# Layer A's normalisers of three chunks spread through DRAM, queries ahead of the output projection, two scratch sets

## The chip, the cores and the metric

The kernel runs on one core of a Trainium2 chip. The core has engines that work side by side and each take their own instructions in order: TensorE (PE, with its weight loads as PEld), VectorE (DVE), ScalarE (ACT), GpSimd (POOL) and SyncE (SP), which here issues the DMA transfers. An instruction that must wait for another engine holds up everything behind it on its own engine. The metric is device time in microseconds of a whole launch; lower is better.

## The reference

The input x has 2048 rows of 1024 values (bf16). Four layers follow one another, A, B, A, B, each with its own layer norm and a residual sum:

```
x = x + A(layernorm(x));  x = x + B(layernorm(x))
x = x + A(layernorm(x));  x = x + B(layernorm(x))
```

Layer A is linear attention with 32 heads of 32 features. Queries and keys go through a small matrix `w_phi` per head; the feature map is the softmax of the result and the softmax of its negative, side by side (64 features):

```
phi_q = concat(softmax(q @ w_phi), softmax(-(q @ w_phi)))      # phi_k alike
kv = sum over rows of phi_k^T v;   z = sum over rows of phi_k
o  = (phi_q @ kv) / (phi_q @ z + 1e-6);   A = o @ wo
```

Layer B is ordinary softmax attention over all 2048 rows, with the same number of heads, and its own `wqkv` and `wo`. The same weights serve both layers A, and both layers B.

## The kernel before

The rows are cut into four chunks of 512 (`c` from 0 to 3); a chunk has four tiles of 128 rows. The residual `xR` stays in SBUF for the whole run. Everything else lives in one SBUF arena of 170 KB per partition, out of which buffers are cut by class, with a quota for each class (`QUOTA`, line 385); PSUM is used as eight banks.

**Who sets the order.** The functions of the kernel don't issue instructions; they hand operations to a planner (`Sched`, lines 62 to 376) with an engine, a duration, what they depend on, their buffers and a priority (a smaller number is more urgent). `Sched.run` lays out a time line by these durations: whenever an engine is free, it takes the ready operation with the smallest priority number for which the buffers can be had. The order that comes out is written into the program and fixed. On the chip every engine follows this order, whether or not the durations hold. A DMA's duration is set by the helper `dma` (line 592): 0.6 us on SP, and a landing 2.25 + kb/210 us later; the broadcasting read below is entered with kb=600.

**One pair of layers**, twice over (`layer` 0 and 1, line 1490). In layer 0 the keys of A are made for all chunks (`a_keys`); in layer 1 only for chunk 3, since the others are made as filler during the attention before (line 1630), along with the query projections of chunk 0 (`q_ahead`, line 943), which wait in DRAM. Then come the queries of A, chunk by chunk at priority `pr = second + 20 * c`:

- `a_queries` (line 959), once for each half `hf` of the eight groups of four heads. PE projects four groups (L600); ACT takes exp of the result and of its negative (L972), which gives the tiles `eq`. PE sums over each head (L983), ACT takes logarithms (L989, L991), DVE subtracts (L993), ACT takes exp (L995): this is the factor `w` by which the negative features have to be scaled, one value for each head and row, held on 8 partitions for each head (16 heads in a half).
- The factor has to stand on all 32 partitions of its head before DVE can multiply. `split_hl` (line 915) writes it as two bf16 parts (L919, L920), and `spread` (line 925) lets PE broadcast these with four matmuls against a selection matrix (L935) into four PSUM banks. DVE multiplies the negative features with them (L1000).
- PE then makes the numerators (L1010), which ACT copies to SBUF (L1014), and the denominators (L1021). ACT takes the denominator's reciprocal by a logarithm and exp (L1026, L1028); `split_hl` and `spread` are used once more, and DVE multiplies the numerators with the result (L1032) into the chunk's output `oc`.
- `a_out` (line 1036) at `pr + PH[1]` projects the output (L600) and adds it to `xR` (L1047); then follow the layer norm for B (`ln_rows`, with transposes through DRAM, L683 and L689), and B's keys and first values at `pr + PH[2]`. With `PH = (1, 22, 43)` and 20 between chunks, chunk c's output projection stands behind the queries of chunk c + 1.

Four chunks, two halves and two normalisers give 16 spreads in each layer A, 32 in all.

**Layer B's attention** (`attention`, line 1183) runs over turns of one chunk and one group. PE makes scores for two or three heads at once (L1209), ACT takes their exp (L1267), and PE multiplies with the values and with ones (L1397). Some score tiles are converted on DVE instead (L1354); `exp_dve` (line 1160) then finishes two of them at a time with bit operations: two masks into the scratch tile `work` (L1171), a product and a sum (L1176). There is one set of `work`, and the planner starts a pair only when the pair before has left it. The quotients of B already go through DRAM: DVE's reciprocals are written to `rd` (L1452) and read back by a DMA that broadcasts four rows to 32 partitions each (L1454), before DVE multiplies (L1459):

```python
bk = dma(prio, lambda r_v=r_v, at_d=at_d: nc.sync.dma_start(
    out=r_v(), in_=at_d.unsqueeze(1).to_broadcast([4, 32, C512])), [aw], [d_b], kb=600)
```

Projections for later groups, the output projection of B (`b_out`, at `P0`, `GAPS`, `OUT_AT`, `GO`) and the keys of the next layer A fill PE's time in between.

## Time and profile before

| | us |
|---|---|
| median of 3 runs (2144.06 to 2144.91) | 2144.25 |
| the profiled execution | 2143.52 |
| its span, first to last instruction | 2141.7 |
| busy in the span: PE, ACT, DVE | 2097.4, 1929.9, 1720.8 |
| first stage of A's queries, about | 147 to 330 |
| second stage of A's queries, about | 1190 to 1365 |

The busy time of PE says little by itself, since matmuls overlap: one lasts some 0.38 us but they start 0.22 us apart. A row of a group has the line, the engine, the operation, output and input tiles with shapes, the count, busy time and mean duration in ns, and the idle time of the engine just before these instructions with what ended it. In a chain of waits each row is a piece of the work that ended last: start, length, what it was. A stretch's row has the busy time of each engine in it, the granted TensorE clock, the mean busy share of the 16 DMA engines, and GB/s.

### The profile page before, as it was taken

How to read it: one execution, taken by the hardware profiler on the slowest of the kernel's cores; microseconds unless marked ns; L12 is line 12 of the kernel's file. 1: busy time of each engine (PE TensorE's matmuls, PEld its weight loads, DVE VectorE, ACT ScalarE, POOL GpSimd, SP SyncE). 2: the span in 40 equal slices, each digit the busy share in tenths (PEclk: the TensorE clock that was granted, in tenths of full speed). 3: DMA queues.
4: the chain of work that ended last, by engine and by line, in shares of the span. 5: the costliest groups of instructions: out<-in, count | busy, mean ns of one | idle time of the engine just before them, and what ended most of it. 6: DMA issues, size and time to landing. Idle time of an engine off the chain costs nothing.

```text
span 2141.7 us, 64212 instructions
## 1 busy us (share of the span) xinstructions
PE 2097.4 (98%) x27375; PEld 795.1 (37%) x27437; DVE 1720.8 (80%) x3151; ACT 1929.9 (90%) x2044; POOL 27.4 (1%) x78
## 2 busy tenths in 40 slices
PE   8999999999999999999999999999999999999999
PEld 5543443333333333333333434533333333333333
DVE  8876553665567899997887876599899999999998
ACT  7437668999999999999999576799999999999998
POOL 1000000000000000000000000000000000000000
PEclk9999999999999999999999999999999999999999
DMA  7820321112233431451456212211111122311111
GB/s 233 164 71 20 86 63 32 32 42 49 65 99 85 123 107 52 120 154 47 108 154 194 78 40 69 70 28 31 36 49 38 45 53 54 84 39 52 54 44 37
DMA packets 255271, 160.73 MB, mean 75 GB/s; under 512 B 147592, under 2 KB 229512, under 8 KB 254984
## 3 DMA queue, kind: packets, MB, share of 16 engines
q1 hardware_dynamic: 254984, 156.62, 27.3%
q8 instruction: 214, 3.51, 0.7%
q14 instruction: 73, 0.60, 0.1%
HBM read 89.72 MB, written 29.87 MB: 56 GB/s over the span
## 4 chain that ended last, share of the span: by engine, by line
PE 57%; ACT 26%; DVE 9%; issue 5%; DMA 2%; POOL 0%; SPq 0%; ACTq 0%; DVEq 0%; POOLq 0%
ACT arena L1267 26%; PE psum L600 19%; PE psum L604 13%; PE psum L1397 11%; PE psum L1209 10%; DVE arena L1354 3%; DVE work L1171 1%; PE psum L1010 1%; DVE work L1176 1%; DVE arena L1176 1%; DMA arena<-rd 1%; DMA arena<-arena 1%; PE psum L855 1%; ACT arena L820 1%; PE psum L935 1%
## 5 line engine op out<-in xcount | busy, mean ns | idle before, releaser
L1267 ACT ACTIVATE arena<-psum 128x1536 bf16<-128x1536 f32 (+1 forms) x1343 | 1580.5, 1478 | 4.7 <-PE psum L1209 2.9
L604 PE MATMUL psum<-arena 128*32 128x512 bf16 (+1 forms) x9536 | 633.1, 365 | 4.2 <-DVE arena L816 1.0
L1397 PE MATMUL psum<-arena 128*32 128x512 bf16 x4096 | 607.5, 382 | 1.9 <-DVE arena L1412 1.6
L1397 PE MATMUL psum<-arena,ones_bf 128*32 128x512 bf16 x4096 | 607.7, 382 | 0.0
L1209 PE MATMUL psum<-arena 32*128 32x512 bf16 x4096 | 527.2, 383 | 25.7 <-ACT arena L1267 20.6
L1354 DVE TENSOR_SCALAR arena<-psum 128x512 uint16<-128x512 f32 x610 | 415.1, 686 | 117.6 <-PE psum L1209 112.9
L600 PE MATMUL psum<-arena 128*128 128x512 bf16 (+1 forms) x1916 | 429.6, 372 | 4.3 <-issue 1.8
L1209 PEld LDWEIGHTS <-arena 32*128 32x128 bf16 x4096 | 161.1, 91 | 559.2 <-issue 555.2
L604 PEld LDWEIGHTS <-arena 128*32 128x32 bf16 x9536 | 206.1, 95 | 255.3 <-issue 161.9
L600 PEld LDWEIGHTS <-arena 128*128 128x128 bf16 x1968 | 186.4, 98 | 215.4 <-issue 17.1
L1397 PEld LDWEIGHTS <-arena 128*32 128x32 bf16 x4096 | 167.2, 95 | 211.6 <-issue 144.0
L1171 DVE TENSOR_SCALAR work<-arena 128x1024 uint16<-128x1024 uint16 (+1 forms) x616 | 237.7, 418 | 5.7
L1176 DVE TENSOR_TENSOR arena<-work 128x1024 bf16<-128x1024 bf16 (+1 forms) x308 | 209.9, 682 | 5.5
L1176 DVE TENSOR_TENSOR work<-arena,work 128x1024 bf16<-128x1024 bf16 (+1 forms) x308 | 209.1, 679 | 0.1
L1397 PEld LDWEIGHTS <-ones_bf 128*32 128x32 bf16 x4096 | 165.9, 95 | 19.1 <-issue 3.3
L820 ACT ACTIVATE arena<-psum 128x512 bf16<-128x512 f32 x80 | 43.6, 595 | 74.4 <-PE psum L600 61.5
L1073 DVE CAST arena<-psum 128x512 bf16<-128x512 f32 (+1 forms) x120 | 69.5, 579 | 41.0 <-PE psum L604 41.0
L824 DVE TENSOR_REDUCE arena<-arena 128x32 f32<-128x1024 bf16 x64 | 77.6, 1213 | 21.4 <-ACT arena L820 21.0
L1412 DVE COPY arena<-psum 128x512 f32<-128x512 f32 x126 | 86.3, 685 | 10.0 <-PE psum L1397 9.8
L972 ACT ACTIVATE arena<-psum 128x512 bf16<-128x512 f32 x112 | 62.0, 605 | 30.4 <-PE psum L600 26.0
L833 DVE TENSOR_TENSOR arena<-psum,arena 128x1024 bf16<-128x1024 f32 x64 | 78.1, 1222 | 5.3 <-PE psum L604 3.1
L645 ACT ACTIVATE arena<-xR 128x1024 bf16<-128x1024 bf16 x40 | 42.3, 1058 | 30.9 <-DVE xR L1047 30.2
(99 smaller groups left out, 1048.4 us busy)
## 6 DMA issues: line engine op xcount, KB each, us to landing
arena<-in_B_wqkv_dram SPq DMA_DIRECT2D x66, 256.0 KB
arena<-rd SPq DMA_DIRECT2D x62, 256.0 KB
xa<-arena SPq DMA_DIRECT2D x48, 256.0 KB
arena<-in_A_wqkv_dram SPq DMA_DIRECT2D x40, 256.0 KB
arena<-in_B_wo_dram SPq DMA_DIRECT2D x40, 256.0 KB
arena<-arena SPq DMA_DIRECT2D x256, 32.0 KB
arena<-wd_k SPq DMA_DIRECT2D x32, 256.0 KB
arena<-arena SPq DMA_DIRECT2D x62, 128.0 KB
```

The source lines that it names most:

```text
L600: nc.tensor.matmul(out_, lhsT=lhsT, rhs=rhs, start=start, stop=stop, skip_group_check=True)
L604: nc.tensor.matmul(out_[ks, :], lhsT=lhsT[:, ks], rhs=rhs, start=start, stop=stop, tile_position=(0, 32 * k), skip_group_check=True)
L824: red = op("DVE", dve_us(1024) + 0.107, lambda ev=ev, sv=sv: nc.vector.reduce_sum(out=sv(), in_=ev().rearrange("p s (h d) -> p (s h) d", d ...
L833: ml = op("DVE", dve_us(1024), lambda vpv=vpv, wv_=wv_, sv=sv: nc.vector.tensor_tensor(out=wv_()[:, :, :, 0:DH], in0=vpv().rearrange("p (h ...
L1073: return soon(op("DVE", dve_us(n), lambda: nc.vector.tensor_copy(out=dst(), in_=src()), [dep], bufs, prio))
L1171: return sch.later("DVE", n * C512 / 3840 + 0.065, lambda: nc.vector.tensor_scalar(out=out_().bitcast(U16), in0=y_v().bitcast(U16), scalar ...
L1176: return sch.later("DVE", n * C512 / 1920 + 0.065, lambda: nc.vector.tensor_tensor(out=out_(), in0=in0(), in1=in1(), op=what), deps, [e_b, ...
L1209: nc.tensor.matmul(out=out_, lhsT=kT[g][1]()[r, pp, d * P:(d + 1) * P], rhs=q_of[(qc, g)][1]()[r, (pp + j // 2) % 2, :], start=True, stop= ...
L1267: ex = make("ACT", act_us(w * C512), lambda: nc.scalar.activation(out=e_v()[:, 0:w * C512], in_=s_v()[:, 0:w * C512], func=ACT.Exp, scale= ...
L1354: pair["got"].append(sch.later("DVE", dve_us(512), lambda: nc.vector.tensor_scalar(out=e_v().bitcast(U16)[:, k, :], in0=s_v(), scalar1=EXP ...
L1397: nc.tensor.matmul(out=a_v()[col:col + 32, :], lhsT=v_v()[:, kc % 4, o:o + DH] if what == 0 else ones_bf[:], rhs=ev()[:, x * C512:(x + 1) ...
L1412: cp = op("DVE", dve_us(512), lambda t_v=t_v, a_v=a_v: nc.vector.tensor_copy(out=t_v(), in_=a_v()), [last], [a_b, t_b], prio - 4)
```

## The change

- `send` is new: the factor (`w`, or the denominator's reciprocal) is written to a DRAM scratch `rw`, one partition of each eight, 16 rows in one DMA; four DMAs then read four rows each, broadcast to 32 partitions a row, into float32 tiles `bw` in SBUF. It takes the place of `split_hl` and `spread` for chunk 0 of layer 0 and chunks 0 and 1 of layer 1 (`FAR = (1, 2)`). DVE's multiplies (L1000, L1032) then read `bw` instead of PSUM.
- `PH` becomes `(1, 42, 63)`: a chunk's output projection and what follows it stand one chunk of queries later.
- `work` has two sets, and two pairs of `exp_dve` may be under way at once. The arena shrinks from 170 to 166 KB. Quotas for `eq`, `ns` and `cw` grow, and `bw` gets 16.
- Some of the planner's durations for short DVE operations are lower, some priorities of filler work move (`QT`, `OUT_AT`, `GO`, `GAPS`), one limit goes from 0 to 1 (`MOST`), and the planner's search through SP's ready list ends early once priorities lie beyond its window; an assertion is added.

```diff
@@ Sched.run
+            assert t < 4000.0
...
+                    if e == "SP" and item[1] > todo[front] + WINDOW:
+                        skipped.append(item)
+                        break
@@ constants
-SBUF_ARENA = 170 * 1024
+SBUF_ARENA = 166 * 1024
...
-         "eq": 12, "ns": 4, "cw": 6, "hl": 6, "oc": 2, "slab": 8, "slabk": 3, "fin": 4,
+         "eq": 20, "ns": 12, "cw": 12, "hl": 6, "oc": 2, "slab": 8, "slabk": 3, "fin": 4,
...
-QT = (188, 300, 310)
+QT = (194.22, 300, 310)
...
+FAR = (1, 2)
...
-OUT_AT = (233.27, 240.45, 284.45)
-GO = 2.34
+OUT_AT = (233.27, 253.5, 284.45)
+GO = 2.55
...
-PH = (1, 22, 43)
+PH = ((1, 42, 63), (1, 42, 63))
...
-GAPS = (1.5, 2.47, 2.87)
+GAPS = (1.5, 2.47, 1.81)
...
-MOST = (lambda i: 0 if i < 1 else 12, lambda i: 16 if i < 1 else 29)
+MOST = (lambda i: 1 if i < 1 else 12, lambda i: 16 if i < 1 else 29)
@@ the kernel
-    work = const.tile([P, 2, max(NB), C512], BF16, tag="work")
+    work = const.tile([P, 2, 2, max(NB), C512], BF16, tag="work")
...
+    rw = dram_p.tile([32 * 16, C512], F32, tag="rw")
+    rw_v = rw[:].rearrange("(t h) n -> t h n", h=16)
+    sent = []
@@ beside spread
+    def send(r_b, r_v, dep, prio):
+
+        at_d = rw_v[len(sent)]
+        sent.append(prio)
+        aw = dma(prio, lambda: nc.sync.dma_start(out=at_d, in_=r_v()[0:P:8, :]), [dep], [r_b], kb=32)
+        got = []
+        for a in range(4):
+            b, v = sb("bw", C512, dt=F32)
+            got.append((b, v, dma(prio + 0.001 * a, lambda a=a, v=v: nc.sync.dma_start(
+                out=v(), in_=at_d[4 * a:4 * a + 4].unsqueeze(1).to_broadcast([4, 32, C512])), [aw], [b], kb=600)))
+        return got
@@ a_queries
-        h_b, h_v, h = split_hl(lm_b, lm_v, w, prio)
         ew, nums = [], []
-        for a, (b_, v_, bm) in enumerate(spread(h_b, h_v, h, prio)):
+        for a, (b_, v_, bm) in enumerate(send(lm_b, lm_v, w, prio) if c < away else spread(*split_hl(lm_b, lm_v, w, prio), prio)):
...
-        k_b, k_v, k = split_hl(r_b, r_v, l4, prio)
-        for a, (b_, v_, bm) in enumerate(spread(k_b, k_v, k, prio)):
+        for a, (b_, v_, bm) in enumerate(send(r_b, r_v, l4, prio) if c < away else spread(*split_hl(r_b, r_v, l4, prio), prio)):
@@ exp_dve
-        x_b = Buf("ps", 0, "xx", [(8,)])
+        x_b = Buf("ps", 0, "xx", [(8,), (9,)])
...
-        x_v = lambda: work[:, 0, 0:n, :]
-        p_v = lambda: work[:, 1, 0:n, :]
+        x_v = lambda: work[:, x_b.at[0] - 8, 0, 0:n, :]
+        p_v = lambda: work[:, x_b.at[0] - 8, 1, 0:n, :]
```

More of the change, by code (lines that the diff above doesn't have):

```diff
@@ L641, in ln_rows @@
                     for h in range(2)]
-                sums.append(op("DVE", 0.2, lambda t=t, b_v=b_v: nc.vector.bn_aggr(
+                sums.append(op("DVE", 0.12, lambda t=t, b_v=b_v: nc.vector.bn_aggr(
                     out=s_v()[:, 2 * t:2 * t + 2], in_=b_v().rearrange("p (h s) -> p h s", s=6)), bn, [b_b, s_b], prio))
@@ L957, in q_ahead, with a_queries @@
                     out=qf_v[:, c, g, :], in_=f_v()), [cp], [f_b], kb=256)
-    def a_queries(c, hf, prio, wq_s, state, o_chunk):
+    def a_queries(c, hf, prio, wq_s, state, o_chunk, away):
         xb, xv, fin = xnA[c]
@@ L1421, in attention @@
                     o_b, o_v = sb("oT", C512)
-                    rc = [op("DVE", 128 * 8 / 960 + 0.12, lambda b=b, T=T, r_v=r_v: nc.vector.reciprocal(
+                    rc = [op("DVE", 128 * 8 / 960 - 0.2, lambda b=b, T=T, r_v=r_v: nc.vector.reciprocal(
                         out=r_v()[hi_, b * P:(b + 1) * P], in_=T[0][1]()[hi_, b * P:(b + 1) * P]),
@@ L1450, in attention @@
                     [T[k][2]], [c_b, T[k][0]], kb=2) for k in range(2) for i in range(2)]
-                rc = op("DVE", 0.27, lambda c_v=c_v: nc.vector.reciprocal(out=c_v(), in_=c_v()), m, [c_b], prio)
+                rc = op("DVE", 0.17, lambda c_v=c_v: nc.vector.reciprocal(out=c_v(), in_=c_v()), m, [c_b], prio)
                 aw = dma(prio, lambda c_v=c_v, at_d=at_d: nc.sync.dma_start(
@@ L1544 @@
             for hf in range(2):
-                a_queries(c, hf, pr + PH[0] * hf, wq_s, state, oc)
-            a_out(c, pr + PH[1], wo_s, oc)
-            xnB[c] = ln_rows(c, 1 + 2 * layer, pr + PH[1] + 1, LN_DVE[layer], c >= LN_PE[layer], c >= LN_PE[layer])
-            b_k(0, c, pr + PH[2], wk0, kT, ANY, "ACT")
+                a_queries(c, hf, pr + PH[layer][0] * hf, wq_s, state, oc, FAR[layer])
+            a_out(c, pr + PH[layer][1], wo_s, oc)
+            xnB[c] = ln_rows(c, 1 + 2 * layer, pr + PH[layer][1] + 1, LN_DVE[layer], c >= LN_PE[layer], c >= LN_PE[layer])
+            b_k(0, c, pr + PH[layer][2], wk0, kT, ANY, "ACT")
             if c == 0:
-                q_of[(0, 0)] = b_q(0, 0, pr + PH[2] + 0.5, wq0, ANY)
+                q_of[(0, 0)] = b_q(0, 0, pr + PH[layer][2] + 0.5, wq0, ANY)
             for t in range(TB):
-                b_v(0, c, t, pr + PH[2] + 1 + 0.1 * t, bv_s[0], vT, ANY, "ACT", (0,) if HALF[layer] else (0, 1))
+                b_v(0, c, t, pr + PH[layer][2] + 1 + 0.1 * t, bv_s[0], vT, ANY, "ACT", (0,) if HALF[layer] else (0, 1))
         gate = []
```

6 lines of the change are left out of this document (3 added, 3 removed).

## The prediction

> **What bounds the kernel now.** I read the page first, then busy time by stage, then the chain of waits inside one stage.
>
> ```profile
> span 2141.7 us, 64212 instructions
> PE 57%; ACT 26%; DVE 9%; issue 5%; DMA 2%; POOL 0%; SPq 0%; ACTq 0%; DVEq 0%; POOLq 0%
> ```
>
> The profiled execution took 2143.52 us around this span; the runs' median, 2144.25, is 0.7 above it. One average hides two regimes, so the second view cuts the span into layer A's query stages (147 to 330 and 1190 to 1365) and the attention stages behind them (columns: stretch, length, busy time of PE, PEld, DVE, ACT, POOL, clock, DMA share, GB/s):
>
> ```profile
> 147.00:330.00 183.00, 181.35 (x1115) 77.64 (x1133) 99.49 (x198) 125.34 (x240) 0.00 (x0) 1.00 0.20 51
> 330.00:1170.00 840.00, 823.04 (x12192) 281.76 (x12191) 631.92 (x1119) 837.19 (x731) 10.14 (x25) 1.00 0.33 90
> 1190.00:1365.00 175.00, 173.58 (x1213) 79.88 (x1232) 117.60 (x219) 113.94 (x225) 2.58 (x8) 1.00 0.21 56
> 1365.00:2141.70 776.70, 760.29 (x11007) 269.33 (x11005) 733.00 (x1393) 763.86 (x678) 0.00 (x0) 1.00 0.17 46
> ```
>
> In the query stages PE is busy for 354.9 of 358 us, while ACT and DVE rest for a third: TensorE sets the pace. In attention ACT has no hole in layer one (837.19 of 840) and only the tail's 12.8 us in layer two. So PE work taken out of a query stage comes off the end, and so does every hole put into it. The change's new operations all lie there. The chain inside the first query stage agrees:
>
> ```profile
> 149.76 5.13 PE psum L600 x23
> 207.04 5.34 PE psum L600 x24
> 244.43 10.74 PE psum L600 x49
> ```
>
> Its long pieces are projections on PE; no transfer is among them. What the change puts there is a transfer.
>
> **The change part by part.**
>
> *TensorE's spreads go.* Three chunks, each with two halves and two normalisers: 12 spreads of 4 matmuls. What one costs, from the order of time:
>
> ```profile
> 1253.17 3.19 PE L600 MATMUL psum<-arena 128*128 128x512 bf16 x14
> 1256.29 0.39 PE L935 MATMUL psum<-arena,selb 32*128 32x512 bf16 x4
> 1256.62 0.60 PE L600 MATMUL psum<-arena 128*128 128x512 bf16 x2
> ```
>
> Fourteen projections keep a pitch of 0.216 us (10.74 us for 49, less one pipeline depth, gives the same), so the last starts at 1255.98; the next one starts at 1256.62, 0.64 later. Without the spread it would be 0.216: a spread costs 0.42. Twelve give 5.1 us; with the whole 0.64 each, 7.7. I take 5.1, the row's own difference.
>
> *VectorE's splitting goes.* 12 casts and 12 subtractions:
>
> ```profile
> L919 DVE CAST arena<-arena 128x512 bf16<-128x512 f32 x32 | 13.6, 425 | 32.2 <-ACT arena L1028 28.8 <-ACT arena L995 3.2
> L920 DVE SCALAR_TENSOR_TENSOR arena<-arena,hl 128x512 bf16<-128x512 bf16 x32 | 24.0, 749 | 0.7
> L1000 DVE TENSOR_TENSOR arena<-arena,psum 128x512 bf16<-128x512 bf16 x64 | 39.9, 683 | 6.5 <-PE psum L935 6.5
> L1459 DVE TENSOR_TENSOR arena<-arena 128x512 bf16<-128x512 f32 x62 | 42.6, 687 | 7.0 <-DMA arena<-rd 5.8 <-DMA arena<-qd 0.8 <-PE psum L1209 0.2
> ```
>
> 12 x (0.425 + 0.749) = 14.1 us of DVE, worth nothing where DVE rests for 84 and 57 us. The 48 multiplies that now read float from SBUF instead of PSUM cost the same (0.683 and 0.687).
>
> *Queries ahead of output projection* (21 to 42 priority units later). No work changes; it can only fill PE's holes, 1.65 + 1.42 us in the two stages. Zero, bound -3.1.
>
> *Two scratch sets.* The attention's groups, and DVE's holes before the last two steps of its exponential (last columns: busy us, mean ns | idle before):
>
> ```profile
> L1267 ACT ACTIVATE arena<-psum 128x1536 bf16<-128x1536 f32 x801 | 1196.3, 1650 | 4.0 <-PE psum L1209 2.2 <-DMA xa<-arena 1.1 <-PE psum L1397 0.6
> L1267 ACT ACTIVATE arena<-psum 128x1024 bf16<-128x1024 f32 x541 | 619.6, 1223 | 0.7 <-PE psum L1209 0.7
> ...
> L1354 DVE TENSOR_SCALAR arena<-psum 128x512 uint16<-128x512 f32 x610 | 415.1, 686 | 117.6 <-PE psum L1209 112.9 <-issue 0.7 <-ACT arena L820 0.4
> L1171 DVE TENSOR_SCALAR work<-arena 128x1024 uint16<-128x1024 uint16 x604 | 234.8, 421 | 5.7
> L1176 DVE TENSOR_TENSOR arena<-work 128x1024 bf16<-128x1024 bf16 x302 | 207.4, 687 | 5.3
> ```
>
> At most 11 us of DVE. Time falls only if units move from ACT to DVE; one costs DVE 0.69 + 0.42 + 0.69 = 1.8 us (conversion, and half of two masks and two combines), so six, at 0.43 us of ACT each (1.650 against 1.223 for three and two banks): -2.6. The limits per turn are the same (0 and 1 alike refuse a pair of two), so I take 0.
>
> *4 KB less arena, retimed fillers, the planner's durations.* Same instructions in another order. ACT's rest in attention, 2.8 + 12.8 us, bounds a gain; nothing bounds a loss. I take 0, and +-3 for the range. The planner's new break and assertion issue nothing.
>
> *The way through DRAM.* Per send: one write of 16 rows, then four reads that each broadcast 4 rows to 128 partitions. The kernel already has that read, form for form, for layer B's normalisers:
>
> ```profile
> 1095.24 3.23 DMA rd<-arena
> ...
> 1098.52 6.20 DMA arena<-rd
> ...
> 1104.81 0.69 DVE arena L1459
> ```
>
> Write 3.28 us to the read's issue; read 6.2 until DVE may use it. The helper that orders the work assumes 0.6 + 2.25 + 600/210 = 5.7 for it, and reads issued 0.6 apart, so an order in which four pieces arrive 5.7, 6.3, 6.9 and 7.5 us after the first issue. For one read that is nearly right. Four together are not in the trace: the closest two are 11.5 us apart:
>
> ```profile
> 907.46 0.57 SPq L1454 DMA_DIRECT2D arena<-rd  x1
> ...
> 918.95 0.59 SPq L1454 DMA_DIRECT2D arena<-rd  x1
> ```
>
> But the read can be seen from within. Two that nothing disturbs, from 1.4 us after their issue (the first one's row), beside the opening loads:
>
> ```profile
> 992.57 0.60 SPq L1454 DMA_DIRECT2D arena<-rd  x1
> ```
> ```profile
> 0.00:50.00 50.00, 43.78 (x467) 28.85 (x474) 41.77 (x80) 34.70 (x65) 5.96 (x19) 0.97 0.82 248
> 993.97:997.12 3.15, 3.15 (x49) 1.08 (x49) 2.55 (x5) 3.15 (x4) 0.00 (x0) 1.00 0.21 81
> 2095.24:2098.50 3.26, 3.06 (x46) 1.08 (x38) 3.23 (x7) 3.26 (x4) 0.00 (x0) 1.00 0.22 79
> ```
>
> 3.15 us at 81 GB/s is 255 KB, one read; share 0.21 of 16 engines is 3.4 of them, where the opening loads use 13. So a read lives on about four engines and fills them for 3.2 us. Ends for four reads: side by side on other engines, as the order assumes (last piece at 6.2 + 1.8 = 8.0), or in single file on the same four (6.2, 9.4, 12.6, 15.8). I take single file: four reads of one form and one queue have nothing to set their engines apart. The last piece then is 8.3 us later than its place in the order, and engines wait in order.
>
> The Trainium skill says this outright (DMA: Bandwidth & Descriptors, Queues, rings and completion order): a copy is split over the largest k up to 16 that divides the outermost sizes of both sides, here 4 and 128, and on the queues of SP the lowest-numbered k are used. The share of 0.21 agrees with k = 4; by the page single file is certain, by the share alone it is likely.
>
> What waits behind a late piece: on DVE the multiply (L1000, L1032), and all that DVE has queued behind it; on PE the numerator (L1010) after L1000. Where each first half and normaliser becomes ready:
>
> ```profile
> 157.21 0.65 ACT L995 ACTIVATE arena<-arena 128x512 f32<-128x512 f32 x1
> 159.78 2.48 DVE L1000 TENSOR_TENSOR arena<-arena,psum 128x512 bf16<-128x512 bf16 x4 [0.67 <-PE psum L935]
> ```
> ```profile
> 176.30 0.69 ACT L1028 ACTIVATE arena<-arena 128x512 f32<-128x512 f32 x1
> ```
> ```profile
> 1189.03 0.65 ACT L995 ACTIVATE arena<-arena 128x512 f32<-128x512 f32 x1
> ```
> ```profile
> 1215.16 0.68 DVE L1000 TENSOR_TENSOR arena<-arena,psum 128x512 bf16<-128x512 bf16 x1
> ```
> ```profile
> 1226.41 0.63 ACT L1028 ACTIVATE arena<-arena 128x512 f32<-128x512 f32 x1
> ```
> ```profile
> 1265.66 0.63 ACT L1028 ACTIVATE arena<-arena 128x512 f32<-128x512 f32 x1
> ```
>
> Layer one, chunk 0: ready 157.9, reads from 161.1. Sixteen reads in file end at 161.1 + 51.2 + 3.0 = 215.3. In the order, the last send starts 7 us later than at 177.0 now (the multiply comes 8.9 after readiness instead of 1.9), and ends 3.3 + 7.5 later: 194.8. So it is between 8.3 (one send's tail) and 20.5 late. Layer two: the first send is covered (ready 1189.7, used at 1215.16). From 1227.0 six sends follow: 1230.3 + 76.8 + 3.0 = 1310.1 against 1265.7 + 7 + 10.8 + 0.6 = 1284.1 for the last: between 8.3 and 26.0 late. PE has no rest to win it back; DVE has a third of its time. I take the middles, 14.4 + 17.2 = 31.6, since DVE catches up on part and PE needs only half of the sends at once.
>
> SP issues 60 transfers more and waits for each write before its reads:
>
> ```profile
> L1454 SPq DMA_DIRECT2D arena<-rd x62: 573/590/662, 368.0 to 2116.1; - x62
> ```
> ```profile
> L1452 SPq DMA_DIRECT2D rd<-arena x62: 320/333/1614, 366.4 to 2114.7; - x62
> ```
> ```profile
> SPq L1454 <- DMA rd<-arena: 31.9, 36, 2.8
> ```
>
> That is 12 x 0.33 + 48 x 0.59 = 32 us of issue and up to 2.8 of waiting per send, ahead of the layer norm's writes and transposes (L683, L689) and the weight slabs. Those are needed a chunk later, and the moved output projections delay the layer norms as well: 0.
>
> Sum: 2143.5 - 5.1 + 31.6 = 2170.0; plus 0.7 for the median: 2171.
>
> **The rivals.**
> *Faster, side by side.* If a read takes whatever engines are free, the last piece is 0.5 us late and the order holds: 2144.25 - 5.1, and up to 3.1 of PE's holes: 2137. For it: a quarter of the engines leaves three quarters idle, at share 0.2. Against: the one form and queue. It decides where a send's four reads land within 8 us. Chance 0.27.
> *Covered.* Single file, but one more chunk of projections (64 x 0.216 = 13.8 us) lies ahead of the first output projection, and only one send's tail reaches PE: 2144.25 - 5.1 + 3 = 2142. For it: layer two's first send waits 25 us anyway. Against: a finished half has the smallest priority number, so its numerator goes next on PE. Chance 0.10, half of it within 0.2%.
> *Full file.* Both upper ends, seven sends in layer two (42 instead of 26): 2144.25 - 5.1 + 20.5 + 42 = 2202. For it: DVE in order. Against: DVE's rest. Holes of 2.6 us between pieces may also slow the clock, which is 1.00 in all four stages and 0.97 in the first 50 us. Chance 0.14. The Trainium skill (TensorE: Matmul & The Clock Gate, Part 1) has the clock halved after an idle window of about 3.4 us; by that, single late pieces alone would not do it, and this trace has no such hole.
> *Attention reordered.* The smaller arena holds back a buffer, or the fillers' new places leave ACT without scores; ACT's 0.43 us per unit is lost for each such unit. +3 to +10, 2150, without any stall for the detour; or the reverse, 2138. Chance 0.07.
>
> **How the numbers follow.** About 0.2% (4 us) is what a measurement of this kernel tells from no change. The forecast has 0.42 (2156 to 2190 its own range), full file 0.14, covered 0.10, side by side 0.27, attention 0.07. Faster: 0.27 + 0.04 + 0.02 = 0.33, one part of it within 0.2%, so 0.32. Same: 0.06. Slower: 0.42 + 0.14 + 0.06 = 0.62. The range reaches to side by side below (2134 with PE's holes and 3 us of order) and towards full file above (2194).
>
> **What would show it.** Right: the reads of the new tensor land about 3 us apart; DVE's L1000 and L1032 have idle time ended by DMA, over 20 us together; PE shows holes before L1010; in layer one the stage behind 147 grows by over 8 us. L935 shrinks from 128 to 80 matmuls and L919 and L920 from 32 to 20 whatever happens. Wrong: L1000 waits under 1 us for its pieces, a stretch over a send has a DMA share near 0.8, and the stages shrink by 2 to 4 us each.

## The result and the profile after

The changed kernel took 2224.16 us (median of 4 runs, 2222.37 to 2226.54) against 2144.58 before: a ratio of 1.037, 95% interval 1.0352 to 1.0388, 79.6 us slower. The forecast was 2171, 26.5 us above the kernel before, with a range up to 2194: the sign is right, the size three times too small.

The page of the changed kernel, its span and the shares of the chain that ended last:

```profile
span 2220.3 us, 64211 instructions
...
PE 48%; ACT 30%; DVE 8%; DMA 7%; issue 6%; SPq 1%; POOL 0%; ACTq 0%; DVEq 0%; POOLq 0%
```

The transfers' share of the chain rose from 2% to 7%, TensorE's fell from 57% to 48%. By stretch (columns as in the prediction: PE, PEld, DVE, ACT, POOL, clock, DMA share, GB/s), with both query stages taken to their new ends:

```profile
147.00:350.00 203.00, 186.85 (x1136) 77.82 (x1134) 95.53 (x190) 129.74 (x242) 0.00 (x0) 0.97 0.23 66
350.00:1193.00 843.00, 822.66 (x12155) 283.32 (x12151) 619.28 (x1099) 833.77 (x727) 10.23 (x25) 1.00 0.32 88
1193.00:1440.00 247.00, 206.49 (x1383) 87.21 (x1380) 129.78 (x239) 133.74 (x263) 2.88 (x8) 0.91 0.36 103
1440.00:2220.30 780.30, 764.08 (x11008) 273.09 (x11006) 712.32 (x1378) 766.13 (x682) 0.00 (x0) 1.00 0.18 45
```

Two things are new, and both are in the query stages. TensorE stands still for 203 - 186.85 = 16.2 us in the first and 40.5 in the second, where it stood 1.65 and 1.42. And its clock, 1.00 in both before, is 0.97 and 0.91, which is worth 0.03 x 203 = 6.1 and 0.09 x 247 = 22.2 us. Together 85 against 3: that is where the 80 us are. The sum counts some 7 us twice, since the clock is also low within some holes (0.63 in the one from 1333.94 to 1341.99, where TensorE stands still anyway); counted once it is 57 of holes and 21 of slow clock, 78.

VectorE's multiplications with the first factors that come through DRAM (order of time; start, length, idle time before):

```profile
165.68 0.69 DVE L1019 TENSOR_TENSOR arena<-arena 128x512 bf16<-128x512 bf16 x1 [9.06 <-DMA arena<-rw]
168.28 0.69 DVE L1019 TENSOR_TENSOR arena<-arena 128x512 bf16<-128x512 bf16 x1 [1.91 <-DMA arena<-rw]
170.85 0.69 DVE L1019 TENSOR_TENSOR arena<-arena 128x512 bf16<-128x512 bf16 x1 [1.89 <-DMA arena<-rw]
173.45 0.69 DVE L1019 TENSOR_TENSOR arena<-arena 128x512 bf16<-128x512 bf16 x1 [1.90 <-DMA arena<-rw]
```

and SP's queue, which sends them:

```profile
157.94 0.58 SPq L953 DMA_DIRECT2D rw<-arena  x1
160.42 4.26 SPq L957 DMA_DIRECT2D arena<-rw  x4
176.33 5.01 SPq L953 DMA_DIRECT2D rw<-arena  x2
181.45 11.89 SPq L957 DMA_DIRECT2D arena<-rw  x8
```

The four reads of a send land 2.6 us apart: single file, as forecast. The next two sends start only at 176.33, 18 us after the first, and both at once, so that eight reads stand in one file. The groups of waits (total, times, longest):

```profile
DVE arena L1050 <- DMA arena<-rw: 50.4, 17, 8.5
DVE arena L1019 <- DMA arena<-rw: 43.0, 20, 9.1
...
PE psum L1029 <- DVE arena L1019: 13.3, 3, 6.3
...
PE psum L608 <- DVE arena L1050: 10.5, 8, 2.2
ACT arena L992 <- DMA rw<-arena: 10.4, 7, 2.5
```

VectorE waits 93 us for pieces, and TensorE waits for VectorE: the numerators (L1029) and denominators (L1040) for the first factors, the output projections (L608) for the second ones. These waits are 32 of the 57 us of holes. Another 14.2 are query projections (also L608) that wait for ScalarE's exponentials (L992) to free a bank, mostly where ScalarE had itself waited for a send's write to land (10.4 us in the last row above; 8.2 us more, once, ahead of the layer norm, L653). In the second stage, TensorE's own rows, of which the last, the longest hole, is of this second kind:

```profile
1279.05 0.59 PE L1029 MATMUL psum<-arena 128*128 128x512 bf16 x1 [6.28 <-DVE arena L1019]
...
1304.35 0.39 PE L608 MATMUL psum<-arena 128*128 128x512 bf16 x1 [1.46 <-DVE arena L1050]
1306.92 0.61 PE L608 MATMUL psum<-arena 128*128 128x512 bf16 x1 [2.19 <-DVE arena L1050]
...
1341.99 3.57 PE L608 MATMUL psum<-arena 128*128 128x512 bf16 x8 [8.05 <-ACT arena L992]
```

### The profile page after: what moved, and what is told of

Same layout as the page of the kernel before. It is cut to its first block, busy times and chain, and to the rows that moved or that the text cites. A ratio compares the mean times of both kernels' runs of the same rounds, so it can differ in the third digit from the quotient of the medians.

```text
span 2220.3 us, 64211 instructions
## 1 busy us (share of the span) xinstructions
PE 2121.4 (96%) x27372; PEld 799.2 (36%) x27372; DVE 1679.8 (76%) x3095; ACT 1935.2 (87%) x2046; POOL 27.5 (1%) x78
## 4 chain that ended last, share of the span: by engine, by line
PE 48%; ACT 30%; DVE 8%; DMA 7%; issue 6%; SPq 1%; POOL 0%; ACTq 0%; DVEq 0%; POOLq 0%
ACT arena L1285 27%; PE psum L612 13%; PE psum L608 13%; PE psum L1415 10%; PE psum L1227 9%; DMA arena<-rw 4%; DVE arena L1372 2%; SPq L957 1%; DVE work L1189 1%; DMA rw<-arena 1%; DVE work L1194 1%; DVE arena L1194 1%; PE psum L863 1%; DMA arena<-arena 1%; ACT arena L828 1%
## 5 line engine op out<-in xcount | busy, mean ns | idle before, releaser
L1415 PE MATMUL psum<-arena 128*32 128x512 bf16 x4096 | 613.8, 382 | 4.7 <-issue 2.2
L1372 DVE TENSOR_SCALAR arena<-psum 128x512 uint16<-128x512 f32 x598 | 407.4, 687 | 125.8 <-PE psum L1227 114.4
L608 PE MATMUL psum<-arena 128*128 128x512 bf16 (+1 forms) x1968 | 452.2, 382 | 25.7 <-ACT arena L992 14.2
L608 PEld LDWEIGHTS <-arena 128*128 128x128 bf16 x1968 | 189.7, 100 | 273.3 <-issue 68.9
L1189 DVE TENSOR_SCALAR work<-arena 128x1024 uint16<-128x1024 uint16 x606 | 240.3, 419 | 3.2
L1194 DVE TENSOR_TENSOR arena<-work 128x1024 bf16<-128x1024 bf16 x303 | 205.9, 680 | 2.9
L1194 DVE TENSOR_TENSOR work<-arena,work 128x1024 bf16<-128x1024 bf16 x303 | 205.8, 679 | 0.0
L992 ACT ACTIVATE arena<-psum 128x512 bf16<-128x512 f32 x112 | 61.9, 606 | 45.9 <-PE psum L608 24.2
L1033 ACT COPY arena<-psum 128x512 f32<-128x512 f32 x64 | 38.0, 594 | 54.7 <-PE psum L1029 39.4
L653 ACT ACTIVATE arena<-xR 128x1024 bf16<-128x1024 bf16 x40 | 42.4, 1061 | 49.1 <-DVE xR L1065 40.9
```

Source lines behind the costliest of these rows:

```text
L608: nc.tensor.matmul(out_, lhsT=lhsT, rhs=rhs, start=start, stop=stop, skip_group_check=True)
L1189: return sch.later("DVE", n * C512 / 3840 + 0.065, lambda: nc.vector.tensor_scalar(out=out_().bitcast(U16), in0=y_v().bitcast(U16), scalar ...
L1194: return sch.later("DVE", n * C512 / 1920 + 0.065, lambda: nc.vector.tensor_tensor(out=out_(), in0=in0(), in1=in1(), op=what), deps, [e_b, ...
L1372: pair["got"].append(sch.later("DVE", dve_us(512), lambda: nc.vector.tensor_scalar(out=e_v().bitcast(U16)[:, k, :], in0=s_v(), scalar1=EXP ...
L1415: nc.tensor.matmul(out=a_v()[col:col + 32, :], lhsT=v_v()[:, kc % 4, o:o + DH] if what == 0 else ones_bf[:], rhs=ev()[:, x * C512:(x + 1) ...
```

## The experiments

Ratios are to the kernel before, on the same chip; "after" is the changed kernel. The constant QT is a due time of the planner; where a version needed another value for the planner to find an order, the diff shows it. The edits are shown in part: quotas of new buffer classes and the size of the DRAM scratch are left out.

**How much is the detour: no chunk, or layer one's alone.**

```
e1  -FAR = (1, 2)  -QT = (194.22, ...)
    +FAR = (0, 0)  +QT = (200, ...)
e5  -FAR = (1, 2)
    +FAR = (1, 0)
```

> The changed kernel with FAR = (0, 0): no chunk goes through DRAM, all the rest of the change stays. (QT is 200 instead of 194.22, because the planner finds no order at 194.22 once the sends are gone.) Theory 1, the four reads of a send run in file on the same few DMA engines and their late pieces stall VectorE and TensorE: both query stages shrink to about 185 and 200 us, no idle time of L1019 or L1050 ends with a DMA, the granted clock is 1.00 again, the time is 2135 to 2160. Theory 2, the new order of queries, the smaller arena and the moved fillers cost most: 2190 or more.

> The changed kernel with FAR = (1, 0): one chunk in layer 0 goes through DRAM, none in layer 1. Theory 1: layer 0's stage stays as long as in the changed kernel (exponentials of attention start near 340 instead of 319), layer 1's stage goes back to some 200 us from 242, and the piece that spilled into the second attention comes back too: 2224 less about 49, 2170 to 2180. Theory 2: over 2195, since the other parts are all there.

Without any detour 2151.15 (1.0033, interval 1.002 to 1.0045); with layer one's chunk alone 2168.35 (1.0114, 1.01 to 1.0128). So the detour costs 73 us, 17 of them by layer one's chunk and 56 by layer two's two; the rest of the change costs 6.8. QT is 200 in e1 and 194.22 in e5 and the kernel after, and no run has its effect alone: the 56 is a difference at one value, the 73, the 17 and the 6.8 are not. e1 lies in theory 1's range, e5 just below it. The query stages without detour have no hole and a full clock:

```profile
147.00:350.00 203.00, 202.96 (x1400) 84.45 (x1397) 105.56 (x206) 142.75 (x253) 0.32 (x1) 1.00 0.18 48
1176.00:1378.00 202.00, 201.95 (x1486) 93.24 (x1477) 135.16 (x252) 136.93 (x273) 2.59 (x8) 1.00 0.30 84
```

**Does layer two's price come from two chunks running into each other?**

```
e14 -FAR = (1, 2)  -QT = (194.22, ...)
    +FAR = (0, 1)  +QT = (200, ...)
```

> FAR = (0, 1): only the first chunk of layer two goes through DRAM. One chunk in layer one alone took 2168, 17 us over none at all (2151); the other two chunks of layer two then took 56. Theory of a price for each send (holes of the same size, chunk by chunk): 2172 to 2182, half of the 56. Rival (the two chunks of layer two run into each other, their sends in one file): 2160 to 2170, like the chunk of layer one, or less because its first send is covered.

2176.62 (1.0146, 1.0131 to 1.0161): 25.5 us for one chunk of layer two, near half of the 56, in the theory's range. The price goes by chunk (e1 and e14 have the same QT). The second stage, the only one touched:

```profile
1175.00:1402.00 227.00, 208.26 (x1474) 94.62 (x1470) 131.34 (x245) 136.80 (x273) 2.59 (x8) 0.96 0.33 94
```

18.7 us of holes and 0.04 x 227 = 9.1 of slow clock. That is somewhat more than layer one's chunk pays (16.2 and 6.1), and half of what the pair pays.

**The landing: four wide reads to a send.** Each read now fills 32 partitions with all four pieces, its 32 repeats outermost; a piece is complete when all four reads have landed.

```
e3  -b, v = sb("bw", C512, dt=F32)                      # one of four
    -out=v(), in_=at_d[4 * a:4 * a + 4].unsqueeze(1).to_broadcast([4, 32, C512])
    +b, v = sb("bw", 4, C512, dt=F32)                   # all four
    +out=v()[32 * h:32 * h + 32], in_=at_d.rearrange("(a h) n -> h a n", h=4)[h].unsqueeze(0).to_broadcast([32, 4, C512])
```

> The changed kernel with the same bytes read in another cut: each of a send's four reads fills 32 partitions with all four pieces, with the 32 repeats as the outermost size, so that it can use 16 DMA engines instead of about 4. Theory 1 (file on few engines): the last piece lands within 8 us of the first issue instead of about 13, a stretch over a send has a DMA share of 0.5 or more, waits of L1019 and L1050 for the reads fall from 93 us to under 25, the clock stays at 1.00 nearly throughout, the time is 2130 to 2160. Theory 3 (any way through DRAM is too long for this order, whatever its rate): waits stay over 60 us and the time over 2190.

2185.92 (1.0203, 1.0189 to 1.0217): the same bytes, 38 us less. Both ranges were missed: VectorE's waits for the reads fell from 93 to 54 us, not below 25. SP's and VectorE's rows of the first send:

```profile
159.03 0.58 SPq L953 DMA_DIRECT2D rw<-arena  x1
161.10 2.20 SPq L955 DMA_DIRECT2D arena<-rw  x4
```
```profile
168.44 2.50 DVE L1018 TENSOR_TENSOR arena<-arena 128x512 bf16<-128x512 bf16 x4 [10.73 <-DMA arena<-rw]
```

All four pieces are there 7.3 us after the first read's issue; in the kernel after the last came at 173.45, 13.0 after its first issue. A stretch within the reads, first of the kernel after, then of this one:

```profile
163.00:170.00 7.00, 7.00 (x29) 2.92 (x27) 1.38 (x2) 3.44 (x7) 0.00 (x0) 0.84 0.26 102
```
```profile
163.00:167.00 4.00, 4.00 (x20) 1.85 (x19) 0.00 (x0) 2.17 (x4) 0.00 (x0) 1.00 0.96 219
```

A quarter of the DMA engines at 102 GB/s, against nearly all of them at 219. The Trainium skill (DMA: Bandwidth & Descriptors, Why a DMA increments its semaphore by 16 and not by 1) splits a copy over the largest k up to 16 that divides the slowest dimensions of both sides; with 4 outermost the trace shows a share of 0.26, near 4 of 16; with 32 outermost, 0.96. Row and rule agree. The stages of this version:

```profile
147.00:350.00 203.00, 194.09 (x1255) 81.67 (x1257) 95.52 (x191) 143.62 (x254) 0.32 (x1) 1.00 0.28 66
1180.00:1398.00 218.00, 198.06 (x1429) 87.05 (x1426) 128.57 (x239) 129.60 (x258) 2.85 (x8) 0.98 0.47 122
```

Holes of 8.9 and 19.9 us, about half of those of the kernel after, and only 4.4 of slow clock.

**Is it an order made for landing times that are too short?** e4 makes the planner count 2.6 us for each broadcasting read, one behind the other (layer B's too); e15 (built on e10, below) adds 3 us to each such read.

```
e4  +if pick.file:
    +    self.narrow = max(self.narrow, t + 1.4) + 2.6
    +    land = max(land, self.narrow + 1.5)
    -QT = (194.22, ...)
    +QT = (198, ...)
e15 -land = max(land, self.wire + 0.6)
    +land = max(land, self.wire + 0.6) + 3.0 * pick.file
```

> The changed kernel, its narrow reads unchanged, but the planner counts them as the trace shows them: one after another, 2.6 us each, the first from 1.4 us after its issue, 1.5 us more to land (for layer B's reads too). QT is 198. Theory 1a, what costs is the order's error: the planner fills the wait with other work, few holes on TensorE, 2140 to 2165. Theory 1b, the file itself costs (48 reads of 2.6 us are 125 us, and too little other work is ready): holes on TensorE remain, 2185 to 2225.

2239.97 (1.0446, 1.0432 to 1.046), slower than the kernel after and above both ranges. A truer plan does not pay.

**Is it the series of the two halves?** In the kernel after the second half's first write comes 18 us or more behind the first half's. The planner hands the buffers of a class out strictly by priority, so the second half's sums wait for a bank that the first half's denominators take first. e6 and e7 give the denominators' bank a class of its own, with narrow and with wide reads:

```
e6, e7  -d_b, d_v = ps("cmp", ANY)
        +d_b, d_v = ps("dn", ANY)
e6      -QT = (194.22, ...)
        +QT = (200, ...)
```

> The changed kernel, narrow reads, with one edit in the planner's classes: the denominators' PSUM bank gets a class of its own, so that the sums of the second half need not wait in the order until the first half's denominators have their bank. (QT is 200.) In the changed kernel the factor of chunk 0's second half is ready 23 us after the first's (156.7 and 179.7), before the change 9.3. Theory H, the sends of the two halves stand in series and each adds its whole way to the chain: now the second factor comes some 10 us after the first, sends overlap, DMA waits of L1019 and L1050 fall below 70 us, 2185 to 2210. Theory F, the file of narrow reads is the bound by itself: over 2212.

> The same class edit together with the reads on 16 engines. If series and file together are the whole cost of the way through DRAM: DMA waits under 25 us, stages as in the run without the detour (attention from about 321, second gap about 202), 2140 to 2160. If something else of the detour costs (SP's order, landing times): over 2170, as with the wide reads alone.

2242.19 (1.0447, 1.0431 to 1.0463) and 2188.26 (1.0196, 1.0181 to 1.0211): no gain, as the rivals had it. But a second lock of the same kind had remained. In e7 the second half's first logarithm (L1008) still comes right behind the first half's denominators' (L1044), whose tile is in the same class:

```profile
172.94 0.60 ACT L1044 ACTIVATE arena<-psum 128x512 f32<-128x512 f32 x1
173.44 0.59 ACT L1008 ACTIVATE arena<-psum 128x512 f32<-128x512 f32 x1
```

So e10 (on e3) and e11 (on the kernel after) free that tile and the second send's landing buffer as well; e12 does it to the kernel before.

```
e10, e11, e12  -d_b, d_v = ps("cmp", ANY)         +d_b, d_v = ps("dn", ANY)
               -r_b, r_v = sb("cw", C512, dt=F32) +r_b, r_v = sb("cwr", C512, dt=F32)
e10, e11       -send(r_b, r_v, l4, prio)          +send(r_b, r_v, l4, prio, "bwr")
```

> The kernel after with wide reads, and with three buffers taken out of the classes in which the planner hands buffers out strictly in order of priority: the denominators' PSUM bank, the denominators' SBUF tile, and the landing buffer of the second send. So the second half's sums, its logarithms, its write and its reads no longer stand behind those of the first half's denominators. Theory (the two halves' sends stand in series because of these orders, and the holes of that series slow the clock): the two halves' first writes come 8 to 11 us apart instead of 23, layer A's first stage (first exponentials of attention 0) falls from 326.4 in the wide version to 318 to 324, the query stage of layer 1 from 218.6 to 203 to 210, total 2150 to 2168. Rival (the price is the landing time itself, each send leaves its hole whatever the order of the halves): first stage 324 or more, total 2180 to 2195, as with wide reads and with the denominators' bank alone.

> The same three buffers in classes of their own, but the reads as in the kernel after, four narrow ones to a send. Theory of the series: the halves overlap, but the eight reads of two sends stand in one file of 2.6 us each, so a part of the price stays: first stage 326 to 334, total 2172 to 2195, that is, about what the prediction had forecast with its overlapped file (2171). Rival (the order of the halves is beside the point): total 2210 to 2235.

> The kernel before with the denominators' bank and tile in classes of their own, no detour. In the kernel before the halves' first writes of the small tile stand 9 us apart already, and the stage is bound by TensorE: theory, nothing is gained, 2140 to 2152. Rival (the order of the halves costs time without any detour too): 2125 to 2138.

2200.27 (1.0255, 1.0238 to 1.0272), 2232.18 (1.0408, 1.0392 to 1.0423) and 2161.41 (1.0076, 1.0061 to 1.0091). In e10 the halves do overlap, with writes 10 us apart:

```profile
158.52 0.58 SPq L953 DMA_DIRECT2D rw<-arena  x1
161.14 2.82 SPq L955 DMA_DIRECT2D arena<-rw  x4
168.45 0.49 SPq L953 DMA_DIRECT2D rw<-arena  x1
```

and yet it is 14 us slower than e3, and e11 8 slower than the kernel after; the other order alone costs the kernel before 16, which neither range for e12 held. e10 lies above both of its ranges, e11 in the rival's. My theory falls: the series is there, but undoing it wins nothing. What it may win by itself can't be told apart from the 16 us that the other order costs.

> The version with wide reads and the three buffers in classes of their own, and the planner is told 3 us more for each read, so that it puts the multiplications where they can run on the chip (write to multiplication 11.7 us in its plan; measured 11.9). Theory (a send is late only because the order was made for times that are too short, other work for TensorE is there): layer two's query stage falls from 232.8 to under 212, total under 2172. Rival (there is no other work within reach, the hole stays wherever the order puts the send): stage 218 or more, total 2180 to 2205.

2198.93 (1.0248, 1.0232 to 1.0263), as e10 and in the rival's range. Its second stage has 20.1 us of holes with the longer times in the plan:

```profile
1182.00:1425.00 243.00, 222.89 (x1746) 101.58 (x1745) 132.59 (x244) 138.21 (x273) 4.29 (x9) 0.97 0.46 119
```

**Is it the slow clock?** Six matmuls on old data ahead of each numerator that waits for a sent factor, in an unchanged order; the numerator overwrites them.

```
e13 +WARM_MM = 6
    +for _ in range(WARM_MM if c < away else 0):
    +    nc.tensor.matmul(n_v(), lhsT=kvm()[:, 2 * g, :], rhs=kvm()[:, 0:4, :].rearrange("p a b -> p (a b)"), start=True, stop=True)
```

> The kernel after, in the same order, with six more matmuls on old data (1.3 us at full clock) on TensorE ahead of each of the 24 numerators whose factor comes through DRAM; the numerator overwrites what they write. In all 31 us of TensorE work that nothing needs, put where the holes are. Theory (about a third of the price, half of the 65 us in which the clock stands at half, comes from the holes slowing the clock): the time at half clock falls from 65 to under 30 us, and the kernel is faster for the added work, 2195 to 2216. Rival (the clock is low only while TensorE waits anyway, and costs nothing): time at half clock falls as well, but the total stays or grows, 2224 to 2255.

2229.12 (1.039, 1.0373 to 1.0408), 5 us above the kernel after:

```profile
147.00:350.00 203.00, 191.38 (x1170) 81.57 (x1171) 95.75 (x190) 128.99 (x240) 0.00 (x0) 0.99 0.22 66
1192.00:1442.00 250.00, 220.05 (x1466) 95.57 (x1467) 128.80 (x237) 131.91 (x260) 2.87 (x8) 0.95 0.36 100
```

My range was missed, the rival's held. The slow clock fell from about 28 us' worth to 2.0 + 12.5, and the holes from 57 to 41.6, but the 31 us of added work took both gains (six matmuls 0.216 us apart, 24 times). That the clock's part would be won if the holes were filled with useful work is not shown.

**Is it a false wait on the write?** In e10 ScalarE's next exponential waits for the write at 10 of the 12 sends. e16 (on e10) and e17 (on the kernel after) keep the small tile until the reads have landed, in case its memory is what the exponential gets. When the wait stayed, e18 (on the kernel after) and e19 (on e16) wrote the whole tile, not every eighth partition.

```
e16, e17       -... [aw], [b], kb=600)
               +... [aw], [b, r_b], kb=600)
e18, e19       -dma_start(out=at_d, in_=r_v()[0:P:8, :])
               +dma_start(out=at_d, in_=r_v())
e18            -in_=at_d[4 * a:4 * a + 4]
               +in_=at_d[32 * a:32 * a + 32:8]
```

> The version with wide reads and three classes of their own, and the small tile that a send writes from is handed back only when the reads have landed, not when the write is planned to be done. In the version without this the next exponential of a query (ScalarE) takes that memory and waits for the write: 25.0 us in 10 waits of ScalarE, 2 to 3.5 us at every send. Theory (this reuse is where the holes come from once the halves overlap): the waits of the exponentials on the write go, first stage under 325, query stage of layer two under 217, total 2160 to 2180. Rival (ScalarE waits then for something else in the same chain; the landing itself is the price): 2190 to 2205.

> The kernel after with the same longer hold on the small tile, nothing else changed. There the exponentials waited 10.4 us in 7 waits on the write, the multiplications 93 us on the reads. Theory (reads in file, one send behind the other, make the price of the kernel after): within 10 us of it, 2214 to 2234. Rival (the reuse of the tile makes the order): under 2205.

> The kernel after in the same order, but a send writes its whole tile (128 rows, 256 KB) to DRAM and the reads pick their 16 rows there. In the kernel after the write takes every eighth partition of the tile; next behind each of the 12 writes ScalarE and VectorE wait for it to land, though they write to other memory. Theory A (the strided source is taken for the whole on-chip memory, so that each write stops the two engines; that is a part of the price): the exponentials' waits on the write (10.4 us in 7) go, total 2196 to 2214. Theory B (those waits lie inside the waits for the reads, 93 us, which stay): 2216 to 2228.

> The version with overlapped halves, wide reads and the longer hold (2183), with the whole tile written. There ScalarE and VectorE wait for each write too, the multiplications of the first half for the write of the second. Theory A: those waits (ScalarE 25.2 us in 10, VectorE 25 us in 7) go, and with them what was left of the price: first stage 320 to 324, query stage of layer two under 210, total 2148 to 2164, near the version with no detour (2151). Rival (the landing itself is the price): 2172 to 2190.

e16 took 2183.28 (1.0177, 1.016 to 1.0194), e17 2234.72 (1.042, 1.0405 to 1.0436). e16 is 17 us faster than e10 and lies between its two ranges, but not for the reason that I gave, since the wait stayed:

```profile
ACT arena L991 <- DMA rw<-arena: 25.2, 10, 4.6
```

In e18 and e19 it is gone, and only the reads are waited for (first e18, then e19):

```profile
DVE arena L1050 <- DMA arena<-rw: 52.8, 20, 7.4
DVE arena L1019 <- DMA arena<-rw: 47.5, 21, 8.8
```
```profile
DVE arena L1018 <- DMA arena<-rw: 18.7, 5, 4.9
DVE arena L1049 <- DMA arena<-rw: 18.5, 4, 10.3
```

So ScalarE and VectorE had waited for a transfer whose source skips partitions, and do not when it takes the whole tile; whether the chip makes this wait or the way the program is built, the rows do not say. But e18 took 2223.0 (1.0357, 1.0342 to 1.0373) and e19 2180.63 (1.0162, 1.0145 to 1.0179), 1 and 3 us less than without it (the 1 is within the spread of the runs): theory A falls in both, the false wait lay inside the wait for the reads. The stages of e19, the best version with all detours:

```profile
147.00:350.00 203.00, 195.82 (x1295) 81.90 (x1316) 99.11 (x193) 139.21 (x249) 0.20 (x1) 1.00 0.29 73
1190.00:1410.00 220.00, 204.10 (x1433) 93.51 (x1457) 127.39 (x236) 138.95 (x274) 3.12 (x8) 0.97 0.47 118
```

**The rest of the change, a part at a time on the kernel before.**

```
e8  -PH = (1, 22, 43)             +PH = (1, 42, 63)
    -QT = (188, ...)              +QT = (194.22, ...)
e9  -Buf("ps", 0, "xx", [(8,)])   +Buf("ps", 0, "xx", [(8,), (9,)])
    -SBUF_ARENA = 170 * 1024      +SBUF_ARENA = 166 * 1024
```

> The kernel before with PH = (1, 42, 63) alone (QT 194.22, at which the planner finds a usable order): the output projection one chunk of queries later, no DRAM, one scratch set. By the prediction no time: 2140 to 2150. If the later projection is what costs the 7 us that are left without the detour: 2150 to 2155.

> The kernel before with two scratch sets and the arena of 166 KB alone. By the prediction no time, 2141 to 2147. If the smaller arena or the second set upsets the attention's order: 2150 or more, with a longer attention stage and fewer units converted on VectorE.

2157.15 (1.0053, 1.0041 to 1.0066) and 2168.41 (1.0111, 1.0096 to 1.0127): 10.6 and 21.9 us slower, each alone and both against the forecast of no time, while the change with both and without the detour is 6.8 slower. Such parts do not add; each makes another order. In e9 the second stage, first before, then e9:

```profile
1170.00:1372.00 202.00, 200.16 (x1449) 93.18 (x1475) 134.92 (x252) 136.11 (x273) 2.72 (x8) 1.00 0.28 79
```
```profile
1176.00:1393.00 217.00, 212.60 (x1595) 98.62 (x1613) 138.92 (x257) 137.36 (x274) 2.60 (x8) 1.00 0.31 89
```

There are 146 more matmuls in it, and 4.4 us of holes in place of 1.8.

**All versions with three detours, by landing and order:**

| | narrow reads | wide reads |
|---|---|---|
| order as the change makes it | 2224 | 2186 |
| denominators' bank free | 2242 | 2188 |
| halves overlapped | 2232 | 2200 |
| longer landing times in the plan | 2240 | 2199 |
| small tile held longer | 2235 | 2183 |
| whole tile written | 2223 | 2181 |
| no detour | 2151 | |

In the narrow column each row is one step away from the kernel after (two of them, the free bank and the longer landing times, with another QT). In the wide column the longer landing times and the longer hold stand on the overlapped halves, and the whole tile on the longer hold. Six versions on either side, and the columns do not meet: narrow is 72 to 91 us over no detour, wide 29 to 49.

**Holes and slow clock against the time**, us, from the two stretches' rows (hole = length less PE's busy time; slow clock = one less the clock, times the length; the kernel after on 147 to 350 and 1193 to 1440, layer one's alone not shown as rows: 203 with 186.90 at 0.97, 201 with 200.70 at 1.00):

| | holes | slow clock | sum | median less 2151 |
|---|---|---|---|---|
| after | 16.2 + 40.5 | 6.1 + 22.2 | 85 | 73 |
| layer one's chunk alone (e5) | 16.1 + 0.3 | 6.1 + 0 | 22 | 17 |
| one chunk of layer two (e14) | 0 + 18.7 | 0 + 9.1 | 28 | 25 |
| wide reads (e3) | 8.9 + 19.9 | 0 + 4.4 | 33 | 35 |
| wide, whole, overlapped (e19) | 7.2 + 15.9 | 0 + 6.6 | 30 | 29 |

The clock has two digits, so its part is good to some 2 us, and some of it stands within holes, as said; the size comes out, and the order but for small differences. Three more versions fit about as well, their stretches taken in the same way (holes plus slow clock): e10 31.6 + 9.0 = 41 against 49, e11 63.5 + 33.1 = 97 against 81, e18 55.5 + 29.7 = 85 against 72.

## Why the prediction was right in sign and wrong in size

- *The bound.* Right. Without detour TensorE is busy 202.96 of 203 us in the first query stage, and what the detour puts into the stages, 78 us of holes and slow clock, comes near to the 73 us that it adds at the end.
- *Spreads and splitting.* TensorE's spread matmuls (L943 now) fell from 128 to 80 as counted. No run has their 5.1 us alone.
- *Queries ahead, two sets, arena: 0, +-3.* Wrong: together 6.8, alone 10.6 and 21.9. I had priced the operations, which hardly change, and not the new order, which costs by itself (e12 changes nothing but two classes of buffers, and costs 16).
- *Single file.* Right: the reads land 2.6 us apart, where 3.2 was worked out from their length. The rival of reads side by side is out for the reads as they are, and e3 shows what a cut that uses all DMA engines is worth: 38 us.
- *Layer one, 14.4 between 8.3 and 20.5.* In its range: 17 by e5. In part that is luck: the four sends did not stand in one file, and the stage has 16.1 us of holes and 6.1 of slow clock, which the term did not hold.
- *Layer two, 17.2 between 8.3 and 26.0: the step that failed.* It measured 56. I had set the end of a file of six sends against the end of the plan, with every send ready nearly as early as before, as if only the last send's lateness mattered and what lay between were caught up. The runs show a price for each chunk: 25.5 for one, 56 for two, 17 in layer one. TensorE stands in holes behind sends of both kinds, because the numerators, denominators and output projections that need them wait in order (L1029 and L608 in the waits above), and nothing wins it back, as that same text said ("PE has no rest to win it back"). Nor were the sends ready early: the reciprocals of the four halves that use sends (ScalarE, L1047) start at 1257.56, 1288.40, 1321.11 and 1353.29, some 32 us apart, where they start some 11 apart without the detour (1233.27, 1244.60, 1256.33 and 1267.30 in e1). The second, for one, follows denominators whose last matmul TensorE could only start at 1286.92, behind the last piece of the send before. How much of the 56 is this slower pace is not shown, since the orders with overlapped halves won nothing. Layer one's own term taken for each chunk, 3 x 14.4 = 43, would have been the consistent sum, and still too small.
- *"Sixteen reads in file".* Wrong. The sends of layer one come as one, two and one, with a pause between them. The planner's strict order of buffers has a part in it; undoing that order lowered nothing.
- *The clock.* Left out of the sum, and given to the rival of the full file as something holes "may" do. It is 21 to 28 us of the stages' loss. Whether it could be won alone stays open after e13. "This trace has no such hole" was a misreading: in its opening the trace of the kernel before has a hole of 3.65 us that ends at 9.84, and its clock is 0.50 from 12 to 14.
- *SP's issue, 0.* Not isolated.
- *The rivals.* Side by side and covered are out. Full file, 2202, was nearer in its number but not in its mechanism; its 42 for seven sends does not follow either, since one send more than six adds 4 x 3.2 to the 26.0, which gives 38.8 and 2198. Attention reordered is no rival for the 80, but was not followed for the 6.8 that the rest of the change costs.

What stays open is why no other work fills the holes. It is not the order of the halves, the plan's landing times, the reuse of the tile or the false wait on the write: each was taken away, or lessened, and the price stayed with the cut of the reads, 72 to 91 us with the narrow and 29 to 49 with the wide ones. What makes up the wide reads' own 29 is not isolated.

## What to carry to other kernels

A value spread through memory costs what the landing of its last piece holds up of everything queued in order behind it. Here that price was paid chunk by chunk (17, 25.5 and, for two, 56 us): cost one chunk with its sends in turn, multiply by the number of chunks, and give nothing back unless the engine that sets the pace has rest in that very stage. Cut a broadcast so that its outermost dimension divides over all DMA engines before anything else is tuned; here the same bytes so cut cost 38 us less in this kernel, though still more than 0.42 us of TensorE for each spread. And where a planner makes the order, run each part of a change alone: parts that cost nothing by their operations moved this kernel by 7 to 22 us.

## What was unexpected of the hardware

The clock fell after shorter holes than I had allowed for. In the kernel after, TensorE's first hole in a query stage is 2.09 us long, the only one in this stretch:

```profile
161.02 5.30 PE L608 MATMUL psum<-arena 128*128 128x512 bf16 x16 [2.09 <-ACT arena L992]
```
```profile
157.00:166.00 9.00, 6.91 (x25) 2.73 (x24) 0.32 (x1) 3.53 (x7) 0.00 (x0) 0.81 0.15 50
```

A mean clock of 0.81 over 9 us is 0.19 x 9 x 2 = 3.4 us at half speed. Taken microsecond by microsecond, the clock is 1.00 up to the end of the hole at 161.02, 0.90 from there to 162, 0.50 from 162 to 165, 0.89 to 166 and 1.00 again: the spell began near 161.8, less than a microsecond behind the end of a hole of 2.09. It does not follow every such hole: those of 2.08 us before 183.32 and of 2.06 before 223.35 left the clock at 1.00. The Trainium skill (TensorE: Matmul & The Clock Gate, Part 1) halves the clock after an idle window of about 3.4 us; 3.4 us is the length that the row shows for the slow spell, but not for the hole before it, and the measurement decides. By that page I had counted late pieces 2.6 us apart as harmless.
